# Another order for the steps of an attention stage spread over four slots, in a fused attention and mixture-of-experts kernel

## The chip, the cores and the metric

The kernel runs on one NeuronCore of a Trainium2 chip. The time is the device time of one execution in microseconds (us). The kernel before takes 812.54 us, the median of three runs (812.51 to 813.44).

## What is computed

Eight batches of 576 tokens, eight heads of 64. Attention is causal over a window of 128 with a linear bias by distance; its output, 512 wide per token, goes to a mixture of eight experts, of which each token uses one. A token may keep the expert of the token before it.

```python
scores = scale * q @ k.T + bias                 # where 0 <= i - j < 128, else -1e9
attn = exp(scores - max); attn = attn / (sum(attn) + 1e-9)
x = attn @ v                                     # heads side by side: 512 per token
...
e = argmax(x[s] @ w_gate) if s == 0 or sigmoid(x[s] @ w_local) < 0.5 else e_of_the_token_before
out[s] = softmax(x[s] @ w_gate)[e] * (relu(x[s] @ w1[e]) @ w2[e])
```

## The kernel before, in words

The attention handles one **pair** of heads at a time: 8 batches x 4 pairs = 32 pairs. Each pair is cut into nine score tiles of 128 rows and 128 or 192 columns. The work on a pair is a set of small steps, methods of `Scores` (L475) and `Weigh` (L530), each a letter and a number:

- S0 to S4 (TensorE, PE): the score matmuls, into four PSUM banks; 34 per pair.
- D0 to D8 (VectorE, DVE): one fused instruction per tile adds the bias, writes the tile `scs` and reduces the row minimum to `mn`; a second, short one reads that out.
- E0 to E8 (ScalarE, ACT): the exponential into the pair's probability buffer `pb` (name `cut`, two of them), with the row sums in `sm`.
- N3 and N8 (L523): the normalisation of tiles 0 to 3 and of 4 to 8. GpSimd (POOL) adds 1e-9 to the sums, VectorE takes the reciprocal `r`, GpSimd multiplies each tile by it.
- U0 to U3 (TensorE): transposes of the probabilities into PSUM tiles `pt` (two); C0 to C3 copy them to `pts`, C3 on VectorE, the others on ScalarE.
- M0 to M4 (TensorE): the matmuls with v, into one PSUM bank `xa`, first for columns 0 to 383, then for the rest; X0 and X1 (ScalarE) copy these to `xT`.
- T0 and T1 (VectorE): 32x32 transposes into the one tile `T`. After T1 of a batch's fourth pair the sync engine's queue (SP) stores all of `T` to `xd` in device memory (L600).

Each engine runs its instructions strictly as written: `InOrder` (L156) chains them, and so most of the attention has the one line L162 in the profile. The order is written by hand: `ORDER` (L60) has one string for each of the four pairs of a batch. The loop over **slots** (L834) runs one string per slot; a step with no mark belongs to this slot's pair, each mark `'` moves it to an earlier pair, and for the steps of `Weigh` one pair more. So the work on one pair lies in slots 0 to 3 from its start (`DEPTH`, L66).

The routing of a finished batch goes in between: a `.` in the string lets the generators `tokens` and `route` (L605, L625) take one step: logits by matmul, the largest of them, a scan over the tokens that carries the held expert on (`hr`), ranks, tables (`tbl`). Nine of these steps put matmuls on TensorE into the one PSUM tile `pk`, each between a VectorE or ScalarE step that feeds it and another that reads it. After the last pair the experts' matmuls follow (L1007 to L1009), with fp32 operands split in two parts (L237, L239).

Of the kernel before, what the change touches and what calls it, by code (L numbers as in the profile page):

```python
# [10 lines left out]
F32 = mybir.dt.float32  # L11
# [39 lines left out]
def windows(nb):  # L51
# [13 lines left out]
]  # L65
DEPTH = 3  # L66
# [8 lines left out]
def moe_attention(ctx, tc, qT, kT_d, vv, wg, wl, w1, w2, out):  # L75
# [232 lines left out]
    with ExitStack() as actx:  # L308
        sp = actx.enter_context(tc.tile_pool(name="asmall", bufs=2))
        ap = actx.enter_context(tc.tile_pool(name="aconst", bufs=1))  # L310
        psc = actx.enter_context(tc.tile_pool(name="psc", bufs=4, space=PS))
# [15 lines left out]

        def load(b):
            (q, q7), v = Q[b % 2], V[b % 2]
            k = sh.tile([P, 4, S], F32, name="kr")  # L330
            for p in range(4):
# [7 lines left out]
                if p == (2 if b == 0 else 1):  # L339
                    nc.sync.dma_start(v[0], vv[b, 0:512].rearrange("(j p) c -> p j c", p=P))  # L340
                    nc.sync.dma_start(v[1][0:64], vv[b, 512:S])
# [133 lines left out]
        class Scores:  # L475


            def __init__(self, b, p, q, q7, k):
                self.p, self.q, self.q7, self.k, self.pb = p, q, q7, k, PB[(4 * b + p) % 2]
                self.mn = sp.tile([P, 9], F32, name="mn")  # L480
                self.sm = sp.tile([P, 9], F32, name="sm")
                self.r = sp.tile([P, 9], F32, name="r")
                self.ps, self.sc = {}, {}
# [4 lines left out]
            def scores(self, i):  # L488
                bank, at = BANK[i]
                return self.ps[bank][:, at:at + self.width(i)]  # L490

            def S(self, j):
                for bank in {0: (0, 1), 2: (2, 3)}.get(j, ()):
                    self.ps[bank] = psc.tile([P, 512], F32, name="sc")
# [813 lines left out]
```

## Time and profile before

| | |
|---|---|
| median of three runs | 812.54 us |
| the profiled execution: its own time, its span | 811.47 us, 809.6 us |
| attention, until the last store of `T` is issued | 338.3 us of the span |
| busy share of the span | PE 90%, DVE 62%, ACT 53%, POOL 50% |
| mean granted clock of TensorE | 0.929 |

The busy share of TensorE is the mean of two stages. The attention ends at 338 us; from 388 us on the experts' matmuls fill TensorE. What the change touches is read from the windows before 338 us, batch by batch. A batch here is the time from one store of `T` to the next.

### The profile page before, as it was taken

Reading aid. Unit: us, or ns where it says so; the run is one execution under the profiler, and the core shown is the slowest. Engines: PE = TensorE matmul, PEld = TensorE weight load, DVE = VectorE, ACT = ScalarE, POOL = GpSimd, SP = SyncE. Lnnn points to the kernel's source line nnn. Section 1 sums busy time; section 2 is a strip of 40 time slices with the busy share of each in tenths; the row PEclk is TensorE's granted clock in tenths of the full one; section 3 lists DMA queues with packets and bytes.
Section 4 is the critical chain, followed back from the end, with each engine's and each line's share of the span. In section 5 each row is a group of like instructions: output and inputs, shape, how many; then the busy total and the mean of one; then the engine's idle time right before and its main releaser. Section 6 shows DMA issues by size and latency. Waiting matters only on the chain.

```text
span 809.6 us, 15889 instructions
## 1 busy us (share of the span) xinstructions
PE 725.5 (90%) x5210; PEld 582.9 (72%) x5210; DVE 500.2 (62%) x1731; ACT 428.4 (53%) x1202; POOL 406.7 (50%) x671
## 2 busy tenths in 40 slices
PE   6788888777787878996999999999999999999996
PEld 3555555545565555675898888898999998888995
DVE  4444656565565566899966459756657657456661
ACT  3576666676666665751454334535545546345550
POOL 8663435343434474677355707365647636705410
PEclk7797979999987887997999999999999999999998
DMA  9343434363625321574455536556657657535520
GB/s 298 112 130 112 148 95 144 107 179 92 188 61 158 130 59 29 168 245 145 143 173 168 167 98 201 177 165 196 220 146 222 213 165 222 175 111 174 187 95 18
DMA packets 65815, 122.20 MB, mean 151 GB/s; under 512 B 14050, under 2 KB 33122, under 8 KB 65731
## 3 DMA queue, kind: packets, MB, share of 16 engines
q1 hardware_dynamic: 55906, 101.27, 40.2%
q0 software_dynamic: 9392, 19.31, 8.1%
q8 instruction: 42, 0.69, 0.3%
q10 hardware_dynamic: 432, 0.59, 0.2%
q14 instruction: 43, 0.34, 0.1%
HBM read 102.14 MB, written 20.30 MB: 151 GB/s over the span
## 4 chain that ended last, share of the span: by engine, by line
PE 61%; ACT 15%; DVE 9%; POOL 6%; issue 6%; DMA 2%; POOLq 0%; ACTq 0%; DVEq 0%
ACT cut L162 11%; PE y L1009 9%; PE y L1008 9%; PE y L1007 9%; PE h L1009 8%; PE h L1007 8%; PE h L1008 8%; PE pt L162 3%; ACT pts L162 3%; PE xa L162 3%; PE sc L162 2%; POOL cut L162 2%; PE pk L162 2%; DMA xd<-T 2%; DVE scs L162 1%
## 5 line engine op out<-in xcount | busy, mean ns | idle before, releaser
L177 POOL DMA_INDIRECT kr<-xd,xidx x142 | 155.9, 1098 | 51.8 <-issue 42.1
L239 DVE TENSOR_TENSOR cut<-wraw,cut 128x512 fp32r<-128x512 f32 x231 | 150.1, 689 | 44.5 <-ACT cut L237 43.1
L162 ACT ACTIVATE cut<-scs,mn 128x192 f32<-128x192 f32 (+1 forms) x288 | 125.0, 436 | 58.4 <-DVE mn L162 47.5
L237 ACT CAST cut<-wraw 128x512 fp32r<-128x512 f32 x218 | 124.2, 618 | 50.1 <-PE y L1009 50.0
L1007 PE MATMUL h<-qx,cut 128*128 128x384 f32 (+7 forms) x472 | 149.6, 317 | 0.0
L1009 PE MATMUL h<-qx,cut 128*128 128x384 f32 (+7 forms) x472 | 149.3, 316 | 0.0
L1008 PE MATMUL h<-qx,cut 128*128 128x384 f32 (+7 forms) x472 | 148.9, 315 | 0.0
L1009 PE MATMUL y<-cut,hl 128*128 128x512 f32 x328 | 129.5, 395 | 0.4 <-DVE hl L1056 0.3
L1008 PE MATMUL y<-cut,hh 128*128 128x512 f32 x328 | 129.4, 394 | 0.0
L1007 PE MATMUL y<-cut,hh 128*128 128x512 f32 x328 | 129.2, 394 | 0.0
L162 POOL TENSOR_SCALAR cut<-cut,r 128x192 f32<-128x192 f32 (+1 forms) x288 | 114.7, 416 | 22.2 <-DVE r L162 13.6
L994 POOL DMA_INDIRECT out<-y,sidx x41 | 43.2, 1054 | 161.4 <-ACT y L1016 133.8
L1055 ACT ACTIVATE hh<-h 128x384 fp32r<-128x384 f32 (+7 forms) x114 | 50.2, 440 | 131.7 <-PE h L1009 131.6
L1056 DVE SCALAR_TENSOR_TENSOR hl<-h,hh 128x384 fp32r<-128x384 f32 (+7 forms) x120 | 58.6, 489 | 83.1 <-ACT hh L1055 81.0
L1007 PEld LDWEIGHTS h<-qx,cut 128*128 128x128 f32 x472 | 90.1, 191 | 5.7
L1008 PEld LDWEIGHTS h<-qx,cut 128*128 128x128 f32 x472 | 89.9, 190 | 5.5
L162 PE MATMUL xa<-pts,cut 128*64 128x128 f32 (+2 forms) x640 | 82.8, 387 | 12.0 <-ACT pts L162 11.9
L1009 PEld LDWEIGHTS h<-qx,cut 128*128 128x128 f32 x472 | 89.9, 190 | 1.8
L162 PE MATMUL pt<-ident,cut 128*128 128x128 f32 x512 | 81.6, 308 | 6.9 <-POOL cut L162 5.1
L162 PEld LDWEIGHTS pt<-ident,cut 128*128 128x128 f32 x512 | 66.9, 159 | 25.9 <-POOL cut L162 18.9
L162 POOL TENSOR_SCALAR r<-sm 128x4 f32<-128x4 f32 x64 | 12.4, 194 | 144.2 <-ACT cut L162 140.9
L162 PE MATMUL sc<-kr,qx 64*64 64x192 f32 (+2 forms) x1088 | 81.9, 369 | 1.6 <-DVE mn L162 1.4
(203 smaller groups left out, 1039.4 us busy)
## 6 DMA issues: line engine op xcount, KB each, us to landing
wraw<-w SPq DMA_DIRECT2D x120, 512.0 KB
xd<-T SPq DMA_DIRECT2D x8, 1152.0 KB
kr<-kT SPq DMA_DIRECT2D x31, 288.0 KB
qx<-qT SPq DMA_DIRECT2D x30, 288.0 KB
cut<-v SPq DMA_DIRECT2D x8, 1024.0 KB
kr<-xd,xidx POOLq DMA_INDIRECT x142, 3.8
qx<-qT SPq DMA_DIRECT2D x16, 64.0 KB
v<-v SPq DMA_DIRECT2D x8, 128.0 KB
```

The costliest lines, as they stand in the source:

```text
L162: ins = getattr(self.engine, name)(*args, **kw)
L177: queued(nc.gpsimd.indirect_dma_start(out=r, out_offset=None, in_=src[0:n, :], in_offset=bass.IndirectOffsetOnAxis(ap=col, axis=0), bounds ...
L237: scalar.copy(c[:, 0, f], raw[:, f])
L239: (pool if 2 * n + f == POOL_CUT else vector).tensor_tensor(c[:, 1, f], raw[:, f], c[:, 0, f], ALU.subtract)
L994: ins = nc.gpsimd.indirect_dma_start(out=out[:, :], out_offset=bass.IndirectOffsetOnAxis(ap=col, axis=0), in_=y, in_offset=None, bounds_ch ...
L1007: nc.tensor.matmul(o, ah, bh, start=start, stop=False)
L1008: nc.tensor.matmul(o, ah, bl, start=False, stop=False)
L1009: nc.tensor.matmul(o, al, bh, start=False, stop=stop)
L1055: now.act.activation(hh, hp, AF.Relu)
L1056: nc.vector.scalar_tensor_tensor(hl, hp, 0.0, hh, ALU.max, ALU.subtract)
```

## The change

Four things change at once.

- The four strings of `ORDER` are new, and a pair's work now lies in slots 0 to 4 (`DEPTH` 4). N is three kinds of step: A (the addition on GpSimd), R (the reciprocal), P (one multiplication per tile). S2 to S4 move from the next slot into the pair's own; E0 to E3 move from the own slot into the next; A, R and P come a slot later than N did; U0, U1, C0, C1, C3, M, X and T one slot later each.
- `ON_VECTOR = {"C0", "X1"}` replaces the test `j == 3`: C0 and X1 run on VectorE, and C3 goes from VectorE to ScalarE.
- `T` is stored in two pieces: columns 0 to 383 after T0 of the fourth pair, the rest after its T1, a slot later. The load of v (`load_v`) comes one slot later than that of q and k.
- M's first and last flags go by whichever step comes first, and every PSUM bank of the scores has a name of its own with one buffer.

```diff
 ORDER = [
...
-    "T1'' S2' S3' S4' . D5' D8' E5' D4' U2' E8' C2' U3' D6' E4' D7' E6' M0' E7' C3' M1' N8' M2' S0 S1 X0' U0 U1 T0' D0 D2 C0 E0 D1 E2 C1 M3' D3 E1 M4' E3 N3 X1' .",
...
+    "C3''' M0''' M1''' E2' M2''' U1'' D8' A8'' E3' D5' X0''' R8'' U0'' . T1'''' P5'' E1' D4' P6'' P7'' D6' E0' T0''' E8' P8'' C1'' E5' D7' M4''' P4'' M3''' . A3' S0 S1 S2 C0'' D2 R3' S3 E4' X1''' E6' E7' . D3 P2' D1 U2'' P1' P0' D0 U3'' C2'' S4 P3'",
...
-DEPTH = 3
+ON_VECTOR = {"C0", "X1"}
+DEPTH = 4
...
-            def N(self, i):
-                g = slice(0, 4) if i == 3 else slice(4, 9)
-                pool.tensor_scalar(self.r[:, g], self.sm[:, g], 1e-9, 1.0, ALU.add, ALU.mult)
-                dve.reciprocal(self.r[:, g], self.r[:, g])
-                for j in range(g.start, g.stop):
-                    pool.tensor_scalar(self.part(j), self.part(j), self.r[:, j:j + 1], 1.0, ALU.mult, ALU.mult)
+            def A(self, g):
+                pool.tensor_scalar(self.r[:, self.group(g)], self.sm[:, self.group(g)], 1e-9, 1.0, ALU.add, ALU.mult)
+            def R(self, g):
+                dve.reciprocal(self.r[:, self.group(g)], self.r[:, self.group(g)])
+            def P(self, i):
+                pool.tensor_scalar(self.part(i), self.part(i), self.r[:, i:i + 1], 1.0, ALU.mult, ALU.mult)
...
-                (dve.tensor_copy if j == 3 else act.copy)(o, self.pt.pop(j).rearrange("k h (x c) -> k h x c", c=P))
+                (dve.tensor_copy if f"C{j}" in ON_VECTOR else act.copy)(o, self.pt.pop(j).rearrange("k h (x c) -> k h x c", c=P))
...
             def T(self, j):
...
+                lo, hi = ((0, 12), (12, SB))[j]
+                dve.transpose(T[:, lo:hi, self.p], self.xT[:, self.p, 32 * lo:32 * hi].rearrange("p (b i) -> p b i", i=32))
+                if self.p == 3:
+                    at = self.b * XR
+                    nc.sync.dma_start(xd[at + P * lo:at + P * hi].rearrange("(b q) c -> q b c", q=P),
+                                      T[:, lo:hi].rearrange("p b k j -> p b (k j)"))
```

**VectorE, one slot.** The numbers behind the names tell the pairs apart: a pair has its own `mn` and `r`, numbered together (`mn_578` and `r_580`; `mn_540` and `r_542`). ISA is the D step. The rows that read out `mn` are left out. Before:

```order
L162 RECIPROCAL r_466<-r_466 128x5
L162 STREAM_TRANSPOSE T_160<-xT_215 128x12x32
L162 ISA scs_662,mn_578<-sc_640,slopes_137 128x192
L162 ISA scs_664,mn_578<-sc_640,slopes_137 128x192
L162 ISA scs_669,mn_578<-sc_641,slopes_137 128x192
L162 ISA scs_676,mn_578<-sc_641,slopes_137 128x192
L162 RECIPROCAL r_580<-r_580 128x4
L162 STREAM_TRANSPOSE T_160<-xT_215 128x6x32
L162 ISA scs_706,mn_578<-sc_696,slopes_137 128x128
```

And now:

```order
L163 ISA scs_620,mn_540<-sc0_603,slopes_137 128x192
L163 RECIPROCAL r_429<-r_429 128x4
L163 COPY xT_215<-xa_594 128x192
L163 ISA scs_631,mn_540<-sc1_605,slopes_137 128x192
L163 ISA scs_634,mn_540<-sc1_605,slopes_137 128x192
L163 ISA scs_643,mn_540<-sc0_603,slopes_137 128x192
L163 ISA scs_670,mn_540<-sc3_615,slopes_137 128x192
L163 ISA scs_674,mn_540<-sc3_615,slopes_137 128x128
L163 RECIPROCAL r_429<-r_429 128x5
L163 STREAM_TRANSPOSE T_160<-xT_215 128x6x32
```

Before, the reciprocal of pair 580 stood right behind the last D step of the same four tiles, with the exponentials and the addition on other engines in between. Now the reciprocals between the D steps of pair 540 are those of the pair before it, and the copy X1 stands on VectorE.

**ScalarE, from the end of one slot into the next.** ACTIVATE is the E step; `pts<-pt` is C, `xT<-xa` is X. Before:

```order
L162 COPY pts_666<-pt_713 128x2x2x128
L162 ACTIVATE cut_140,sm_579<-scs_711,mn_578 128x128
L162 ACTIVATE cut_140,sm_579<-scs_725,mn_578 128x192
L162 ACTIVATE cut_140,sm_579<-scs_728,mn_578 128x192
L162 COPY xT_215<-xa_731 128x384
L162 COPY pts_780<-pt_765 128x2x2x128
L162 ACTIVATE cut_143,sm_692<-scs_776,mn_691 128x192
L162 ACTIVATE cut_143,sm_692<-scs_778,mn_691 128x192
L162 COPY pts_780<-pt_770 128x2x2x128
```

And now:

```order
L163 COPY pts_703<-pt_751 128x2x2x128
L163 COPY pts_703<-pt_760 128x2x256
L163 ACTIVATE cut_143,sm_654<-scs_734,mn_653 128x192
L163 ACTIVATE cut_143,sm_654<-scs_746,mn_653 128x192
L163 COPY xT_215<-xa_783 128x384
L163 ACTIVATE cut_143,sm_654<-scs_749,mn_653 128x192
L163 ACTIVATE cut_143,sm_654<-scs_758,mn_653 128x192
L163 ACTIVATE cut_143,sm_654<-scs_796,mn_653 128x192
L163 COPY pts_844<-pt_791 128x2x2x128
L163 ACTIVATE cut_143,sm_654<-scs_800,mn_653 128x128
```

C2 and C3 now stand back to back at the slot's border, all nine E steps of one pair lie between there and the next C2, and X1 is gone from ScalarE.

**SP, around the store of a batch.** Before:

```order
L334 DMA qx_135<-qT 128x576
L340 DMA cut_141<-v 128x4x512
L341 DMA v1_142<-v 64x512
L600 DMA xd_75<-T_160 128x18x128
L334 DMA qx_135<-qT 128x576 x3
```

And now:

```order
L340 DMA qx_135<-qT 128x576
L611 DMA xd_75<-T_160 128x12x128
L331 DMA cut_141<-v 128x4x512
L332 DMA v1_142<-v 64x512
L611 DMA xd_75<-T_160 128x6x128
L340 DMA qx_135<-qT 128x576 x2
```

The first two thirds of `T` go out ahead of the load of v, the last third behind it.

## Rows read from the trace of the kernel before

**Rows 1.** Busy time by window (the queries for stretches of the span). The first line is a slot without routing, the next five each run from one store of `T` to the next, the last three are the way over to the experts' stage. Columns: the stretch and its length, busy us of each engine (x instructions), granted clock of TensorE, DMA share, GB/s.

```profile
41.93:49.97 8.04, 6.77 (x83) 4.81 (x82) 4.03 (x24) 6.06 (x23) 5.74 (x17) 1.00 0.68 227
...
58.66:99.78 41.12, 33.51 (x339) 22.46 (x338) 24.04 (x129) 26.11 (x97) 18.14 (x70) 0.83 0.43 130
99.78:140.53 40.75, 33.58 (x342) 22.62 (x338) 23.62 (x128) 26.11 (x97) 16.35 (x46) 0.83 0.40 122
140.53:178.32 37.79, 28.67 (x342) 19.56 (x338) 23.42 (x128) 25.99 (x97) 16.33 (x46) 1.00 0.44 130
178.32:216.57 38.25, 29.80 (x342) 20.30 (x338) 23.21 (x128) 26.00 (x97) 16.14 (x46) 0.96 0.42 131
216.57:257.48 40.91, 34.27 (x346) 23.52 (x338) 23.82 (x128) 26.24 (x97) 16.60 (x46) 0.83 0.36 111
...
338.30:360.00 21.70, 20.56 (x142) 16.09 (x138) 19.92 (x57) 12.77 (x30) 16.64 (x13) 1.00 0.88 286
360.00:388.00 28.00, 20.63 (x117) 16.80 (x115) 26.26 (x111) 8.39 (x17) 19.66 (x19) 0.82 0.45 138
388.00:809.60 421.60, 414.05 (x2266) 367.80 (x2263) 257.34 (x514) 193.80 (x376) 204.03 (x190) 0.99 0.53 164
```

**Rows 2.** The transposes into `T` and their stores over the whole span: durations in ns (least, median, most), start of the first and of the last.

```profile
L162 DVE STREAM_TRANSPOSE T<-xT x64: 345/459/578, 29.2 to 337.9; 128x384 f32<-128x384 f32 x32, 128x192 f32<-128x192 f32 x32
L600 SPq DMA_DIRECT2D xd<-T x8: 377/378/387, 58.7 to 338.3; - x8
```

**Rows 3.** The chain of work that ended last, inside the slot without routing from 41.93 to 49.97 us: start, us, what.

```profile
42.20 0.25 DVE scs L162
...
42.87 0.62 ACT cut L162 x3
43.50 0.47 ACT pts L162
43.97 1.28 ACT cut L162 x6
45.24 0.08 issue
45.32 0.21 POOL r L162
45.53 0.02 issue
45.55 0.20 DVE r L162
45.75 0.08 issue
45.84 1.92 POOL cut L162 x5
```

**Rows 4.** Who waited for whom in the batch from 140.53 to 178.32 us: engine and tile, what it waited for: us in total, times, longest us.

```profile
DVE r L162 <- POOL r L162: 11.5, 8, 2.1
ACT pts L162 <- PE pt L162: 4.6, 4, 2.2
...
PE pk L162 <- DVE tbl L162: 2.5, 1, 2.5
PE pk L162 <- DVE hr L162: 2.3, 2, 1.9
...
PE pk L162 <- DVE rcb L162: 1.6, 1, 1.6
...
PE pk L162 <- DVE ro_all L162: 1.4, 2, 0.9
...
PE xa L162 <- ACT pts L162: 1.1, 2, 0.6
DVE T L162 <- DMA xd<-T: 1.0, 1, 1.0
```

**Rows 5.** Groups of instructions by shape in the same batch: count, busy us, mean ns of one, idle time before them.

```profile
L162 ACT COPY pts<-pt 128x512 f32<-128x512 f32 x12 | 6.8, 570 | 4.6 <-PE pt L162 4.6
...
L162 DVE CUSTOM_DVE_ANT_0 scs<-sc,slopes 128x192 f32<-128x192 f32 x24 | 7.5, 344 | 0.0
...
L162 DVE COPY pts<-pt 128x512 f32<-128x512 f32 x4 | 2.7, 686 | 0.0
...
L162 ACT COPY xT<-xa 128x192 f32<-128x192 f32 x4 | 1.2, 297 | 0.0
```

**Rows 6.** The chain of work that ended last, around the second store of `T`: start, us, what.

```profile
99.78 7.08 DMA xd<-T
...
106.96 0.58 DVE T L162
```

**Rows 7.** Busy time by window, columns as in Rows 1: two stretches right before the granted clock fell, and the two that followed them at the lower clock.

```profile
66.80:70.20 3.40, 1.51 (x10) 1.01 (x10) 1.59 (x13) 2.54 (x10) 0.19 (x1) 1.00 0.36 94
70.20:80.40 10.20, 8.47 (x66) 5.62 (x70) 5.99 (x30) 6.22 (x23) 4.07 (x12) 0.50 0.00 1
...
107.80:111.20 3.40, 1.63 (x12) 1.13 (x10) 1.51 (x12) 2.55 (x10) 0.42 (x2) 0.99 0.35 89
111.20:121.40 10.20, 8.80 (x70) 5.96 (x74) 5.68 (x27) 6.54 (x25) 3.54 (x10) 0.50 0.01 2
```

More of the change, by code (lines that the diff above doesn't have):

```diff
@@ L338, in load @@
                         nc.sync.dma_start(q7[hs, :, hs], qT[b, :, hs, 448:512].rearrange("p d q -> d p q"))
-                if p == (2 if b == 0 else 1):
-                    nc.sync.dma_start(v[0], vv[b, 0:512].rearrange("(j p) c -> p j c", p=P))
-                    nc.sync.dma_start(v[1][0:64], vv[b, 512:S])
+                if p == 2 and b == 0:
+                    load_v(b)
             return q, q7, k, v
@@ L479, in __init__ @@
                 self.p, self.q, self.q7, self.k, self.pb = p, q, q7, k, PB[(4 * b + p) % 2]
-                self.mn = sp.tile([P, 9], F32, name="mn")
-                self.sm = sp.tile([P, 9], F32, name="sm")
-                self.r = sp.tile([P, 9], F32, name="r")
+                self.mn, self.sm, self.r = (sp.tile([P, 9], F32, name=n, bufs=4) for n in ("mn", "sm", "r"))
                 self.ps, self.sc = {}, {}
@@ L489, in scores @@
                 bank, at = BANK[i]
+                if bank not in self.ps:
+                    self.ps[bank] = psc.tile([P, 512], F32, name=f"sc{bank}")
                 return self.ps[bank][:, at:at + self.width(i)]
             def S(self, j):
-                for bank in {0: (0, 1), 2: (2, 3)}.get(j, ()):
-                    self.ps[bank] = psc.tile([P, 512], F32, name="sc")
                 if j == 4:
@@ L572, in M @@
             def M(self, j):
+                half = j // 3
+                first = half not in self.o
+                if first:
+                    self.o[half] = pxa.tile([P, 512], F32, name="xa")
+                o = self.o[half]
                 if j == 0:
-                    self.xa = pxa.tile([P, 512], F32, name="xa")
-                    self.mult(self.xa[:, 128:384], 4, 4, 1, True, False)
+                    self.mult(o[:, 128:384], 4, 4, 1, first, False)
                 elif j == 1:
-                    self.mult(self.xa[:, 256:384], 8, 2, 2, False, False)
+                    self.mult(o[:, 256:384], 8, 2, 2, first, False)
@@ L587, in X @@
             def X(self, j):
+                copy = dve.tensor_copy if f"X{j}" in ON_VECTOR else act.copy
                 if j == 0:
-                    act.copy(self.xT[:, self.p, 0:384], self.xa[:, 0:384])
+                    copy(self.xT[:, self.p, 0:384], self.o[0][:, 0:384])
                 else:
-                    act.copy(self.xT[:, self.p, 384:S].rearrange("p (s q) -> p s q", q=64),
-                             self.xb[:, 0:192].rearrange("p (s q) -> p s q", q=64)[:, ::-1])
+                    copy(self.xT[:, self.p, 384:S].rearrange("p (s q) -> p s q", q=64),
+                             self.o[1][:, 0:192].rearrange("p (s q) -> p s q", q=64)[:, ::-1])
@@ L613, in tokens @@
                 yield
-                act.copy(part[:, lo:lo + n], pk[:, :n])
+                (dve.tensor_copy if "part" in ON_VECTOR else act.copy)(part[:, lo:lo + n], pk[:, :n])
                 yield
@@ L787, in early, with over @@
             known.append(e)
+        def over(kind, n):
+            return all((a, n) in emitted for a in atoms if a[0] == kind)
         def gathers():
@@ L803, in turns @@
             for t in range(r.n):
-                while taken.count(t) < 4 or ("S4", 4 * NB - 5) not in emitted:
+                while taken.count(t) < 4 or not over("S", 4 * NB - 5):
                     yield
@@ L812, in turns @@
             yield from W.split(tp.tile([P, 2, 2, DM], F32R, name="xT"), act, dve)
-            for what in (("M4", 4 * NB - 5), ("U3", 4 * NB - 2), ("M4", 4 * NB - 1)):
-                while what not in emitted:
+            for what in (("M", 4 * NB - 5), ("U", 4 * NB - 2), ("M", 4 * NB - 1)):
+                while not over(*what):
                     yield
                 yield from W.split(W.room(), act, dve)
-        known, taken, routed, read, emitted = [], [], [], [], []
+        known, taken, routed, read, emitted = [], [], [], [], set()
         rows0 = [Rows(4 * KS * e, KS * e, 4 * k, idx0, n) for e, (k, n) in enumerate(EARLY)]
@@ L821, in moe_attention @@
         pairs = {}
+        atoms = {a.strip("'") for a in ORDER[0].split()}
         LATE = 4 * EARLY[0][1] + 4
@@ L864, in moe_attention @@
                 loaded = load(b + 1)
+            if p == 2 and b + 1 < NB:
+                load_v(b + 1)
         run(chain(prep[";"], prep[":"], prep[","], side))
```

37 lines of the change are left out of this document (17 added, 20 removed), and 6 rows, old and new, of the table ORDER.

## The prediction

> **What bounds the kernel now.** I read the busy time by window first, since the change touches the attention alone. The experts' stage has TensorE busy for 414.05 of its 421.60 us [rows 1]: nothing there can be gained by another order ahead of it, but an attention that ends sooner lets it begin sooner. The attention is the part before the last store at 338.3 us; the eight stores lie between 58.7 and 338.3 [rows 2], so a batch takes (338.3 - 58.7) / 7 = 39.95 us. In no window of a batch is an engine full: in the one with the granted clock at 1.00 throughout, TensorE is busy for 28.67 of 37.79 us, ScalarE 25.99, VectorE 23.42, GpSimd 16.33 [rows 1]. So the batch is bound by waits between engines, not by an engine.
>
> Which waits, the chain of one slot without routing tells [rows 3]: D on VectorE, the exponentials on ScalarE, then the addition on GpSimd (0.21), the reciprocal on VectorE (0.20), the five multiplications on GpSimd (1.92). The table of waits shows the price in a batch: VectorE stands for 11.5 us in front of its eight reciprocals [rows 4], which is most of its idle 37.79 - 23.42 = 14.4 us. VectorE works strictly in its order, so the next D steps, and with them the next exponentials, stand behind each reciprocal. That is a ring: E, A, R, D, E. The routing's VectorE steps stand behind it too, and TensorE then waits for them: 2.5 + 2.3 + 1.6 + 1.4 = 7.8 us, and 1.1 for C [rows 4], together 8.9 of its 9.1 idle us.
>
> **The change, part by part.**
>
> *A, R and P apart, a slot later.* The instructions and their number stay the same. Between the last E of a group and its A, and between A and R, there are now steps of other pairs on each of the three engines, so R should find its sums ready: I take the 11.5 us as gone from VectorE's path. Bounds: nothing of it goes if A is late on GpSimd (it stands behind the four P of the group before), all of it goes if A is on time. GpSimd is busy for 16.33 of 37.79 us [rows 1], so I take the second. P is then followed by U half a slot later or more; GpSimd's 1.92 us for five tiles [rows 3] fits there.
>
> *Copies.* X1 leaves ScalarE: -4 x 0.297 = -1.2 us a batch [rows 5]. On VectorE it costs between 0.344 (an instruction of the same 128x192 from PSUM) and 0.686 us (a copy of 128x512) [rows 5]; I take 0.37, near the one of the same width: +1.5 us a batch, at most +2.7. C0 comes to VectorE and C3 goes to ScalarE: both are 128x512, 0.686 and 0.570 us each [rows 5], so the swap costs neither engine anything. The sums per batch become ScalarE 25.99 - 1.2 = 24.8, VectorE 23.42 + 1.5 = 24.9. Both stay below TensorE's 28.67, and that covers the copies; if TensorE's floor were lower, they would be the next bound.
>
> *The store in two pieces.* The second store took 7.08 us and T0 of the next pair began right after it [rows 6]; VectorE's wait for it in the full-clock batch is 1.0 us [rows 4]. Now each piece has until the same T step of the next pair, a slot later. A slot without routing is 8.04 us now [rows 1] and I expect some 7 after; two thirds of the store need about 4.7 (estimate, in proportion to 7.08). So the wait goes; it is inside VectorE's idle time, and I count nothing for it by itself. Eight more DMAs on SP cost it 8 x 0.38 = 3 us in all [rows 2], on a queue that waits for others most of the time. What stands behind the second piece are loads of q for a batch that is four slots away.
>
> *One slot more.* A fifth slot for each pair adds a drain slot at the end. Its last steps are M, X and T alone, and the experts' first matmuls may run beside them; at the start, S and D of more pairs run ahead while GpSimd still builds the bias tables. I count 0, bounds -2 and +4 us (half a slot of 8.04).
>
> *The sum.* TensorE becomes the fullest engine: 28.67 us per batch at the full clock. Of its waits I keep the two that are round trips through the one tile `pk` and that no order shortens, the table (2.5) and the scan (2.3): 28.67 + 4.8 = 33.5 us. The others (1.6 + 1.4 + 1.1) were VectorE and ScalarE running late, and go. Over the seven batches between the stores: 7 x (39.95 - 33.5) = 45.2 us. The slots before the first store have no routing: from the first T at 29.2 to 58.7 [rows 2] there are three and a half, of 8.04 us, with TensorE busy for 6.77 [rows 1]; at 7.2 they give 3.5 x 0.84 = 2.9. Together 48.1 us. The hand-over to the experts, 338 to 388 us, is led by VectorE (26.26 of 28.00 busy in its second part [rows 1]) with work that the change leaves alone, so it moves forward as a whole. Against the profiled execution: 811.47 - 48.1 = 763.4; it stands 1.07 below the median of the runs, so 764.5 against that. I say **764**.
>
> *A rule weighed.* That sum takes TensorE's matmul time as a floor. The same rows show its weight loads busy for only 19.56 of the 37.79 us [rows 1]. The Trainium skill (Perfetto Trace Analysis, Identifying the Most-Contended Engine) says that matmul busy time is a poor measure of how near TensorE is to its limit, and that the busy share of the weight loads should be used instead. By that rule TensorE has more room than I gave it, and the sum would go by VectorE's 24.9; that is the first rival.
>
> **The rivals.**
>
> 1. *TensorE's floor is lower than its busy time.* Then the batch is VectorE's 24.9 us plus the same 4.8 of round trips: 29.7 us, a gain of 7 x 10.25 + 3 = 75, time **738**. For it: the busy time overlaps and may hold waits. Against it: in the experts' stage the matmuls are 98% busy and nothing else bounds there, and three engines with 24.8 to 28.7 us of work each would have to interlock with 5 us of slack.
>
> 2. *The clock still falls.* In three of the five batches the granted clock is 0.83 on average, which is one third of the time at 1.2 GHz instead of 2.4, and they take 40.75 to 41.12 instead of 37.79 us [rows 1]. Before each fall TensorE was busy for only 1.51 and 1.63 of 3.40 us [rows 7]; it was waiting for the routing's `rcb`, and then ran at the lower level for 10 us. If such gaps remain, a batch costs 40.75 - 37.79 = 3.0 us more: 36.5, a gain of 7 x 3.45 + 3 = 27, time **785**. At worst TensorE's full extra busy time counts, 33.58 - 28.67 = 4.9 [rows 1]: 38.4, time 799. For it: the routing keeps its gaps of some 2 us in one place. Against it: TensorE has less idle time around them. The Trainium skill (TensorE: Matmul & The Clock Gate, A second HAM failure mode: psum-queue depth-cycling) describes a kernel whose short idle spells between groups of matmuls keep sending the clock back and forth; by that rule this rival is what happens, and the rows of the batches at 0.83 agree with it, the one at 1.00 does not.
>
> 3. *Slower: the routing waits grow.* The new order fills ScalarE and VectorE (24.8 and 24.9 us) and the routing's steps are still thrown in by the same dots, in the same strict queues. Nine of them put matmuls on TensorE. Now six of the waits show up, 7.8 us, 1.3 each [rows 4]. If all nine wait as long, and C's waits grow by as much as they are, the waits are 9 x 1.3 + 2 x 1.1 = 13.9: a batch of 42.6, 7 x 2.65 - 3 = 16 us slower, time **828**. It decides from 39.95 - 28.67 = 11.3 us of TensorE waits a batch on; they are 9.1 now. For it: each of the steps has a reader on a queue that is now fuller. Against it: what made them late, 11.5 us of reciprocals, is what the change takes out.
>
> 4. *The change does not do what it says.* A is behind the P steps on GpSimd, R still waits for it, and a ring of the same length stays with one slot more: **812** to 816.
>
> **How the numbers follow.** My forecast, a batch of 32 to 35.5 us (750 to 778), has a chance of 0.62; rival 1 0.12, rival 2 0.18, rival 3 0.05, rival 4 0.03. The first three are faster, which makes 0.92. What a measurement can tell from no change is about 0.2%, 1.6 us; rival 4 holds most of what lies within it. The range takes in rival 1 and rival 2 at its first price, with the bounds of the extra slot: 734 to 792. Outside are the worst of rival 2 and rivals 3 and 4, under 2 in 10.
>
> **What would show it.** In the profile after: the distance of the stores of `T` about 33 us; VectorE's wait for `r` of GpSimd near 0 in a batch; TensorE's idle time in a batch about 5 us, with the table and the scan as its leading waits; VectorE busy for about 25 us, ScalarE for a little less; no wait of T for its store; the way from the last store to the full experts' stage about 50 us as now. The prediction is wrong if the reciprocals still wait for some us, if the granted clock in the batches stays near 0.83, or if the distance from the last store to the end grows by what the attention has won.

## The result, and the profile of the changed kernel

The changed kernel takes **722.88 us** (median of four runs, 721.73 to 723.69) against 812.52: a ratio of 0.8907, 95% interval 0.8868 to 0.8946. Here and below a median counts every run, while a ratio leaves out runs over 1.5% above the fastest of their kernel, so that the two need not agree to the last tenth of a per cent. The forecast was 764 with a range of 734 to 792: the sign and the way were right, the gain was nearly twice as large, and the time lies below the range. The profiled execution has a span of 721.1 us against 809.6, 88.5 less, of which the forecast had 48.1.

The transposes into `T` and their stores over the whole span (columns as in [rows 2]); the stores are now two per batch:

```profile
L163 DVE STREAM_TRANSPOSE T<-xT x64: 326/466/579, 30.2 to 250.6; 128x384 f32<-128x384 f32 x32, 128x192 f32<-128x192 f32 x32
L611 SPq DMA_DIRECT2D xd<-T x16: 359/380/388, 48.7 to 251.0; - x16
```

The last store goes out at 251.0 us instead of 338.3. From there to the end of the span it is 721.1 - 251.0 = 470.1 us, and was 809.6 - 338.3 = 471.3 [rows 2]. So 87.3 of the 88.5 us lie in the attention, and the way over to the experts moved forward as a whole.

Busy time by window (columns as in [rows 1]); the first three run from the second store of one batch to that of the next, the last three are the way over and the experts' stage:

```profile
53.17:79.89 26.72, 26.23 (x335) 18.52 (x335) 23.92 (x132) 24.22 (x92) 16.46 (x46) 1.00 0.59 180
...
107.26:134.41 27.15, 26.66 (x340) 18.98 (x339) 23.81 (x132) 24.83 (x94) 16.43 (x46) 1.00 0.59 181
...
161.53:192.09 30.56, 29.20 (x365) 20.35 (x363) 24.94 (x139) 26.50 (x100) 16.36 (x46) 1.00 0.57 176
251.30:272.00 20.70, 19.32 (x132) 15.38 (x132) 18.28 (x53) 12.12 (x27) 14.33 (x13) 1.00 0.80 257
272.00:300.00 28.00, 20.62 (x122) 16.87 (x121) 27.05 (x114) 9.08 (x18) 19.88 (x19) 0.88 0.46 140
300.00:721.10 421.10, 413.25 (x2260) 366.92 (x2258) 256.43 (x513) 193.28 (x375) 204.95 (x190) 1.00 0.53 164
```

A batch takes 27.15 us where the one at the full clock took 37.79 [rows 1]. TensorE is busy for 26.66 of them, 98%. The other engines' busy times are close to what they were (VectorE 23.42 to 23.81, ScalarE 25.99 to 24.83, GpSimd 16.33 to 16.43): the same work, without the holes. Note TensorE's own: about the same number of matmuls at the same granted clock, yet 28.67 us before and 26.66 now. Its busy time before was not all work. The batch at 161 us has 365 matmuls instead of 340, as preparation for the experts comes in; the two behind it take some 31 and 28 us.

The chain of work that ended last, in the batch from 107.26 us (shares by line, then the first pieces: start, us, what), is now for the most part TensorE's own queue:

```profile
by line: PE pt L163 26.5%; PE xa L163 22.6%; PE sc L163 19.4%; PE pk L163 12.1%; DVE scs L163 8.7%; DVE ro_all L163 3.7%; DVE T L163 2.7%; issue 1.4%; DVE pts L163 1.2%; DVE r L163 1.0%; DVE tbl L163 0.5%; DVE tz L163 0.3%; DVE mn L163 0.3%
...
107.78 0.25 PE pk L163 x8
108.03 1.23 PE xa L163 x12
109.27 0.59 PE pk L163 x4
109.85 0.87 PE pt L163 x8
110.72 0.11 PE pk L163
110.83 0.81 PE xa L163 x12
111.64 1.35 PE sc L163 x32
113.00 0.31 PE pk L163 x4
113.31 1.02 PE pt L163 x8
```

Up to 126.67 us group follows group with no other engine between; in the chain of before [rows 3] ScalarE, GpSimd and VectorE took turns. The routing's matmuls (`pk`) stand among the attention's. It is not TensorE alone: VectorE has the 5.3 us from 126.68 to 131.98, and in the batch ahead of this one, of nearly the same length, VectorE's D steps (22.4%) and ScalarE's exponentials (13.1%) lead the chain. In the four batches from 53.17 us TensorE's four groups (`pt` 20.2, `xa` 18.1, `sc` 14.8, `pk` 11.7%) make 65% of it; in the four of before from 58.66 us the same four make 18%, and ScalarE's exponentials alone 32.5%.

Who waited for whom, from 50 to 250 us, about seven batches (columns as in [rows 4]); VectorE, then TensorE, then ScalarE:

```profile
DVE L L163 <- PE pk L163: 14.9, 7, 2.9
...
DVE r L163 <- POOL r L163: 1.2, 2, 0.7
...
PE pk L163 <- DVE hr L163: 3.4, 3, 2.4
PE pk L163 <- DVE tbl L163: 2.9, 6, 0.6
...
ACT cut L163 <- DVE mn L163: 0.2, 1, 0.2
```

The reciprocals' wait, 11.5 us in one batch before [rows 4], is 1.2 in seven. The table's, 2.5 in one batch, is 0.4; the scan's (`hr`) is under 0.5. No T waits for its store.

Groups by shape in the batch from 107.26 us (columns as in [rows 5]):

```profile
L163 ACT COPY pts<-pt 128x512 f32<-128x512 f32 x13 | 7.3, 579 | 0.1
L163 DVE COPY pts<-pt 128x512 f32<-128x512 f32 x4 | 2.7, 679 | 0.0
...
L163 DVE COPY xT<-xa 128x192 f32<-128x192 f32 x4 | 1.4, 338 | 0.0
```

X1 on VectorE takes 338 ns (0.37 us was taken), and the copies of 128x512 cost what [rows 5] had for them.

### The profile page after: what moved, and what is told of

Same layout as the page of the kernel before. It is cut to its first block, busy times and chain, and to the rows that moved or that the text cites. A ratio compares the mean times of both kernels' runs of the same rounds, so it can differ in the third digit from the quotient of the medians.

```text
span 721.1 us, 15988 instructions
## 1 busy us (share of the span) xinstructions
PE 678.9 (94%) x5210; PEld 558.0 (77%) x5210; DVE 504.4 (70%) x1763; ACT 419.5 (58%) x1170; POOL 409.3 (57%) x671
## 4 chain that ended last, share of the span: by engine, by line
PE 75%; DVE 10%; POOL 6%; issue 5%; ACT 3%; DMA 1%; POOLq 0%; DVEq 0%
PE y L1025 10%; PE y L1024 10%; PE y L1023 10%; PE h L1023 10%; PE h L1025 9%; PE h L1024 9%; PE pt L163 5%; PE xa L163 5%; PE sc L163 4%; DVE scs L163 3%; PE pk L163 3%; POOL cut L163 2%; ACT cut L163 2%; POOL qx L163 1%; DVE cut L240 1%
## 5 line engine op out<-in xcount | busy, mean ns | idle before, releaser
L163 POOL TENSOR_SCALAR cut<-cut,r 128x192 f32<-128x192 f32 (+1 forms) x288 | 116.4, 422 | 55.9 <-DVE r L163 32.7
L1024 PEld LDWEIGHTS h<-qx,cut 128*128 128x128 f32 x472 | 89.6, 190 | 5.6
L163 PE MATMUL pt<-ident,cut 128*128 128x128 f32 x512 | 73.3, 285 | 10.7 <-POOL cut L163 10.6
L163 PEld LDWEIGHTS pt<-ident,cut 128*128 128x128 f32 x512 | 56.8, 144 | 31.3 <-POOL cut L163 20.3
L1025 PEld LDWEIGHTS y<-cut,hl 128*128 128x128 f32 x328 | 61.5, 188 | 15.3 <-DVE hl L1072 2.0
L163 DVE CUSTOM_DVE_ANT_0 scs<-sc,slopes 128x192 f32<-128x192 f32 x224 | 68.9, 334 | 5.3 <-ACT cut L163 3.4
L163 PE MATMUL xa<-pts,cut 128*64 128x128 f32 (+2 forms) x640 | 70.2, 337 | 0.6 <-ACT xT L163 0.6
```

The lines of the kernel that those rows point to most:

```text
L163: ins = getattr(self.engine, name)(*args, **kw)
L1024: nc.tensor.matmul(o, ah, bl, start=False, stop=False)
L1025: nc.tensor.matmul(o, al, bh, start=False, stop=stop)
```

## The experiments

Every kernel's median is in us, its ratio is to the kernel before, timed with it. In the last three groups of runs the experts' stage took some 60 to 95 us longer in every kernel, in the kernel before too (872.92 to 906.22), while the attention seems not to have: a kernel run in two of these groups, with 561.2 and 536.8 us from its last store to the end, issued its last store at 282.7 and 282.8 us. No kernel was profiled both in one of these groups and outside them. So all kernels are set side by side by the start of the last store of `T` in their profiles. For the store in two pieces alone that does not do: its profile is of a run of 817.36 us at a granted clock of 0.919, far from its median.

| kernel | last store, us | median (of before) | ratio, interval |
|---|---|---|---|
| before | 338.3 | 812.52 | 1 |
| before + store in two pieces | 344.2 | 809.31 (813.34) | 0.9935 [0.9892, 0.9978] |
| before + ring out | 307.5 | 780.44 (813.34) | 0.9608 [0.9572, 0.9645] |
| ... and store in two pieces | 297.5 | 770.59 (811.72) | 0.949 [0.9433, 0.9546] |
| ... and T later | 282.8 | 816.45 (872.92) | 0.933 [0.9255, 0.9405] |
| ... and S2 to S4 ahead | 280.5 | 815.30 (872.92) | 0.9349 [0.9307, 0.9391] |
| changed | 251.0 | 722.88 (812.52) | 0.8907 [0.8868, 0.8946] |
| changed, old copies | 249.3 | 721.19 (813.21) | 0.8877 [0.8823, 0.8931] |
| changed, old copies, T behind X | 266.4 | 803.75 (872.92) | 0.9222 [0.9176, 0.9269] |
| changed, ring back | 262.7 | 734.61 (813.34) | 0.9039 [0.9006, 0.9073] |
| changed, one store | 283.7 | 752.50 (813.21) | 0.9257 [0.9199, 0.9314] |
| changed, ring back, one store | 292.8 | 762.09 (811.72) | 0.937 [0.9313, 0.9428] |
| changed, dots four steps later | 259.0 | 813.02 (906.22) | 0.8994 [0.8902, 0.9086] |
| changed, dots four steps earlier | 256.3 | 811.59 (906.22) | 0.8983 [0.8877, 0.909] |

### The ring of the reciprocals, out and back

Out, in the old order (`mn`, `sm` and `r` have four buffers each there, as in the changed kernel):

```diff
-    ... D5' D8' E5' D4' ... M1' N8' M2' ... C0 E0 D1 E2 ... E3 N3 X1' .
+    ... D5' D8' E5' R3' P0' P1' P2' P3' D4' ... M1' A8' M2' ... C0 E0 R8' P4' P5' P6' P7' P8' D1 E2 ... E3 A3 X1' .
```

> The kernel before, three slots deep as it was, same copies and store; only N is split into A, R and P, and R with its P steps stands later: R3 in the next slot behind two D steps, R8 behind D0, D2 of the next pair. Ring theory: VectorE's 11.5 us a batch in front of the reciprocals go to under 3, and the batch falls from 40 to 33 to 36 us: 770 to 785. Rival (the deeper pipeline is what counts): the waits move to TensorE's U behind P and the time falls by under 10 us (803 to 812).

Back, in the new one:

```diff
-    ... D8' A8'' E3' D5' X0''' R8'' ... E0' ... A3' S0 ... D2 R3' ... E6' E7' D3 ...
+    ... D8' E3' D5' X0''' ... E0' A3' R3' ... S0 ... D2 ... E6' E7' A8' R8' D3 ...
```

> The changed kernel, with A and R put right behind the last exponential of their group again (A3, R3 behind E0; A8, R8 behind E7), all else in its place. Ring theory: VectorE waits again in front of the reciprocals, 6 to 11 us a batch, D and E behind it are late, and the batch goes from 27.2 to 32 to 36 us: 757 to 785. Rival (depth of five slots covers it): under 5 us slower (723 to 728).

Out alone, it gave 32.9 us. Back alone, it cost 11.7. Both theories of the second run missed: the ring costs there, but a third of what it costs in the old order. Waits of VectorE with the ring back, from 60 to 250 us:

```profile
DVE r L163 <- POOL r L163: 10.2, 19, 1.1
```

The reciprocals wait again, yet 10.2 us in 6.6 batches, where the old order had 11.5 in one [rows 4]. My reading is that a reciprocal that waits closes a ring only if ScalarE then waits for the next D. In the new order E0 to E3 come a slot after their D steps, and ScalarE has their results lying ready (its wait for `mn` is 0.2 us above, and with the ring back none is listed), so it goes on and the sums come soon after.

### The store of T

The piece alone in the old order:

```diff
-                    if self.p == 3:
-                        nc.sync.dma_start(xd[self.b * XR:self.b * XR + XR]..., T...)
+                if self.p == 3:
+                    lo, hi, at = ((0, 12), (12, SB))[j] + (self.b * XR,)
+                    nc.sync.dma_start(xd[at + P * lo:at + P * hi]..., T[:, lo:hi]...)
```

> The kernel before, with the store of T in two pieces (columns 0 to 383 after T0 of the fourth pair, the rest after its T1) and nothing else. If the store is a part of the gain by itself, VectorE's wait of T for its store goes, 1.0 us a batch at the full clock and 2.2 us in the batch of the second store: 7 to 15 us faster (798 to 806), the more so since the wait is followed by D and E. If it is hidden in the ring E, A, R, D anyway, 0 to 3 us.

It gave 0.65%, 5.3 us, with an interval of 1.8 to 8.8: between the two cases, and the interval reaches into both. The times of single runs of this kernel spread from 801.15 us at a granted clock of 0.964 to 817.36 at 0.919, so that nothing finer can be read from it. With the ring out it is clearer:

> The kernel before with the reciprocals a slot later (780.4 us) and the store in two pieces. With the ring out alone, VectorE's T waited 2.7 us for its store in a batch. Theory, the wait for the store was covered by the ring and counts as soon as the ring is gone: 7 x 2 to 2.7 us less, 761 to 767. Rival, other waits of the old order take its place: 776 to 781. Far below 761 would say that nothing else of the new order matters.

780.44 fell to 770.59: 9.9 us, where the theory had 14 to 19. What stands in its place is shown below. And taken back from the new order:

```diff
-                if self.p == 3:
+                if self.p == 3 and j == 1:
...
-                                      T[:, lo:hi]...)
+                                      T...)
```

> The changed kernel with one store of T after T1, instead of two pieces. T0 of the next pair then waits for a store that was issued a few us before: the store took 7.08 us before, a slot takes 6.8 us now, and T1 stands about a third of a slot into it. If VectorE's wait is on the path: 3 to 5 us in each of seven batches, 15 to 35 us longer (738 to 758). If the slack of VectorE (3.3 us a batch) takes most of it: 0 to 5 us longer. The prediction counted 0 for this part.

29.6 us longer. VectorE's longest wait in that kernel from 50 to 275 us, and two places of its chain of work:

```profile
DVE T L163 <- DMA xd<-T: 26.6, 7, 5.1
```

```profile
85.35 0.26 DVE T L163
85.63 6.78 DMA xd<-T
92.51 0.58 DVE T L163
...
116.97 0.26 DVE T L163
117.25 7.12 DMA xd<-T
124.47 0.58 DVE T L163
```

T1, the store, T0 of the next pair: the store stands on the path in full, in each of the seven batches (5.51 to 8.04 us); before, it stood there twice, with 7.08 [rows 6] and 6.00. It takes about as long as it did, but T0 now comes sooner after T1: T waits for it seven times, 26.6 us, and before four times, 4.5. The granted clock in these batches is 0.89 to 0.95, where the changed kernel has 1.00 in six of seven, so that a part of the 29.6 us may be the clock; the two were not told apart. The same part that was worth some 5 us in the old order is worth 30 in the new one.

### Ring and store both back

> The changed kernel with both taken back: A and R right behind the exponentials of their group, and one store of T. What is left of the change is the order over five slots and the copies. Theory, the parts add: 734.6 + 29.6 = 764, 758 to 770. Rival 1, they stand in each other's time, since both keep VectorE waiting: 750 to 757. Rival 2, each protected the other and without both the batch falls back to the kernel before: over 780.

762.09: the parts add in the new order (734.61 + 29.6 = 764). So with the ring back the store still costs 27.5 us (762.09 - 734.61). Left over are the order over five slots and the copies, and they alone make 50 of the 89.6 us. What goes with that order, a name of its own for each PSUM bank of the scores and the later load of v, was not tried apart from it.

### The copies, and which engine is full

```diff
-ON_VECTOR = {"C0", "X1"}
+ON_VECTOR = {"C3"}
```

> The changed kernel with the copies on their old engines: X1 and C0 on ScalarE, C3 on VectorE. ScalarE gets 1.2 us a batch more (24.8 to 26.0 of 27.15), VectorE 1.4 less. The prediction's view (the copies are covered by TensorE): 0 to 3 us longer. Rival, ScalarE at 26 of 27.15 us has no slack for its place in the order, so that the copies were a needed part of the gain: 5 to 12 us longer, 728 to 735.

721.19: the copies are no part of the gain; ScalarE's 1.2 us more a batch was hidden, and VectorE's 1.4 less gave nothing that can be told. This version and the changed one can't be told apart (their intervals overlap); no better version came out of the experiments.

More work for one engine at a time in the changed kernel: S4's matmul issued twice, T1's transpose made twice, a further copy of 192 columns on ScalarE.

```diff
-                    pe.matmul(self.scores(6), ...)
+                    for _ in range(2):
+                        pe.matmul(self.scores(6), ...)
```

> The changed kernel with the score matmul of step S4 issued twice per pair, into the same place: TensorE gets two more matmuls of 192 columns per pair (one step S4 holds one call; some 0.33 us a pair at the rate of its neighbours, 32 pairs: 10.6 us in all), the other engines nothing. Theory, TensorE is now what bounds the attention: 8 to 12 us longer, 731 to 735 against 722.9. Rival, a ring of waits or VectorE or ScalarE bounds it and TensorE has room: 0 to 3 us longer.

```diff
-                dve.transpose(T[:, lo:hi, self.p], ...)
+                for _ in range(1 + j):
+                    dve.transpose(T[:, lo:hi, self.p], ...)
```

> The changed kernel with the 32x32 transpose of step T1 made twice: VectorE gets one more instruction of 0.34 us per pair, 10.9 us over 32 pairs. Theory, TensorE bounds: VectorE goes from 23.8 to 25.2 us of work in a batch of 27.15 us, so it is hidden: 0 to 3 us longer, at most 726. Rival, VectorE bounds or lies on a ring: 8 to 11 us longer, 731 to 734.

```diff
                     copy(self.xT[:, self.p, 0:384], self.o[0][:, 0:384])
+                    copy(self.xT[:, self.p, 0:192], self.o[0][:, 0:192])
```

> The changed kernel with one more copy of 192 columns on ScalarE per pair, right behind X0: 0.30 us a pair, 9.5 us over 32 pairs. VectorE and TensorE, given about as much, each became 5.3 us longer, half of it. Theory, the three engines are so full that each one's work counts: 4 to 6 us longer, 727 to 729. Rival, ScalarE has room (it took 1.2 us a batch more with the old copies at no cost): 0 to 2 us, 721 to 725.

Measured 728.14, 728.31 and 723.51. Four batches of each, store to store, first the changed kernel, then with more for TensorE, for VectorE and for ScalarE (columns as in [rows 1]):

```profile
53.17:161.53 108.36, 106.42 (x1349) 75.46 (x1349) 95.45 (x528) 98.72 (x371) 65.67 (x181) 1.00 0.59 180
```

```profile
52.75:164.85 112.10, 110.77 (x1383) 81.37 (x1382) 95.26 (x528) 98.52 (x372) 65.69 (x181) 1.00 0.58 175
```

```profile
52.84:165.08 112.24, 107.23 (x1344) 75.91 (x1344) 100.85 (x544) 99.89 (x372) 65.82 (x181) 1.00 0.57 175
```

```profile
51.96:160.15 108.19, 106.33 (x1351) 75.67 (x1351) 95.43 (x528) 101.61 (x388) 65.98 (x181) 1.00 0.60 181
```

TensorE's added work was less than I had put down: 4.35 us of busy time in four batches, where 16 pairs at 0.33 are 5.3. Of it 3.74 us appear in the time, 86%. So TensorE has next to no room in these batches. But of VectorE's 5.40 us 3.88 appear too, 72%, although VectorE is idle for 12% of the time: it has slack in sum and little at the places where TensorE needs its result (TensorE's weight loads for `sc` waited 5.6 us for `mn` there). The two set the pace together, as in the chain above. ScalarE's extra copies are 16 of 319 ns in four batches, 5.1 us, and those batches take 108.19 us against 108.36: nothing of it appears. The expectation that VectorE's would be hidden was wrong.

This holds for these four batches. From the fifth on, up to the last store, the changed kernel, then with more for TensorE and for VectorE:

```profile
161.53:251.00 89.47, 79.65 (x924) 56.38 (x922) 76.28 (x388) 71.84 (x253) 59.69 (x130) 0.98 0.46 143
```

```profile
164.85:254.90 90.05, 81.88 (x942) 59.53 (x940) 75.44 (x388) 71.63 (x252) 59.56 (x130) 0.98 0.45 142
```

```profile
165.08:256.30 91.22, 80.17 (x920) 56.85 (x919) 80.42 (x400) 71.66 (x252) 58.94 (x130) 0.96 0.45 140
```

TensorE is busy for 89% there, and of its 2.23 us more 0.58 appear, of VectorE's 4.14 us 1.75 (and of ScalarE's 2.72 us 1.08): these three batches still wait for other things. Over the whole kernel the two additions cost 5.3 and 5.4 us, not the 8 to 12 that a full TensorE would have made of its own.

### What of the order over five slots does it

With ring and store settled, the old order has a batch of 34.34 us (columns as in [rows 1]):

```profile
157.84:192.19 34.35, 29.36 (x339) 19.72 (x338) 23.60 (x128) 25.76 (x97) 16.36 (x45) 1.00 0.47 143
```

VectorE's waits in it from 60 to 250 us:

```profile
DVE T L162 <- ACT xT L162: 31.8, 27, 1.7
DVE hr L162 <- ACT hold L162: 9.5, 12, 1.1
```

T stands right behind X, and VectorE's queue behind T. Moved apart in the old order, and together in the new one (with old copies):

```diff
-    T1'' S2' ... D6' E4' ... T0' D0 D2 ... D3 E1
+    S2' ... D6' T1'' E4' ... D0 D2 ... D3 T0' E1
```

> The kernel before with the reciprocals a slot later and the store in two pieces (770.6 us), and now T0 and T1 put some steps further behind X0 and X1: T0 behind D3 instead of ahead of D0, T1 behind D6 of the next slot instead of at its head. VectorE waited for xT for 31.8 us in the 190 us from 60 to 250, 5.7 in a batch of 34.3. Theory, these waits are on the path and are what the longer distances of the new order remove: 2 to 5 us less in each of seven batches, 735 to 757. Rival, the waits move on to the next steps, since in the old order every engine waits for every other: 764 to 772.

> The same kernel as with T moved alone. Its first run was on another chip, on which the experts' stage took 90 us longer in every kernel; its last store of T was issued at 283 us of the span. If the attention is the same on both chips: last store at 281 to 285 us, time 750 to 757.

```diff
-    ... X0''' R8'' U0'' . T1'''' ... E0' T0''' ... X1''' E6' ...
+    ... X0''' T0''' R8'' U0'' . ... E0' ... X1''' T1''' E6' ...
```

> The changed kernel with the copies on their old engines (721.2 us), and T0 and T1 put right behind X0 and X1, as near as in the old order. VectorE then waits in front of T for ScalarE. Theory, the distance of T from X is a main part of what the order over five slots gives: 2 to 6 us more in each of seven batches, 735 to 763. Rival, the slack of VectorE (some 4 us a batch here) takes it: 721 to 727.

> The same kernel as the changed one with old copies and T right behind X. Its last store of T was at 267.5 us on the other chip, against 249.3 in the kernel without this edit. If the attention is the same on both chips: time 736 to 742, 15 to 20 us over 721.2.

The times expected of the two second runs were missed by some 60 us, since the experts' stage was long again. The last store came 15 us earlier in the first (297.5 to 282.8; 844.23 and 816.45 us, 0.9354 and 0.933 of the kernel before), 17 to 18 us later in the second (249.3 to 266.4 and 267.1; 833.42 and 803.75). So this one distance is worth 15 to 18 us in either order. In its place, in the old order, came VectorE's wait for TensorE:

```profile
DVE scs L162 <- PE sc L162: 25.1, 23, 3.1
DVE hr L162 <- ACT hold L162: 7.3, 12, 0.9
```

which the next edit took aim at:

```diff
-    S2' S3' S4' . D5' ... U0 U1 D0 ...
+    . D5' ... U0 U1 S2 S3 S4 D0 ...
```

> The old order with the reciprocals a slot later, the store in two pieces, T0 and T1 further behind X0 and X1, and now S2, S3 and S4 ahead of M3 and M4 in TensorE's queue, behind U1 of their own slot, as the new order has them in the own slot. With T moved alone a batch took 31.7 us and VectorE's longest wait was scs for sc, 25.1 us in 190, 4.2 in a batch. Theory, the gain of the new order is a sum of such lengthened distances: this takes 1.5 to 4 us more off a batch, 10 to 28 us off the time with T moved alone (that was 0.935 of the kernel before, about 753 to 760 here), so 728 to 748. Rival, the wait moves on: within 5 us of the kernel with T moved alone.

The wait fell, the time hardly (last store 282.8 to 280.5): the rival was right. In the same 190 us it is now

```profile
DVE L L162 <- PE pk L162: 11.1, 11, 1.8
DVE scs L162 <- PE sc L162: 9.3, 12, 1.1
DVE hr L162 <- ACT hold L162: 7.7, 12, 0.9
DVE oh_all L162 <- PE pk L162: 4.9, 6, 0.9
```

many small waits on several engines, and the batch looks like this:

```profile
147.41:178.82 31.41, 29.40 (x339) 19.44 (x340) 23.24 (x129) 25.55 (x98) 16.41 (x46) 1.00 0.51 156
```

TensorE is "busy" for 29.40 of 31.41 us with as many matmuls as take 26.66 in the changed kernel. (The profiles of T moved alone and of this kernel are of runs of 821.35 and 824.72 us, above their medians.) The other 30 us, from 280.5 to 251.0, I have not split further: what is left in the new order is E0 to E3, the whole of U, C and M at longer distances from what feeds them, and the dots. That E0 to E3 are the part which keeps ScalarE from waiting fits its wait for `mn` (8.1 us in 190 in this kernel, 0.2 in 200 in the changed one), but it was not tried alone.

### The places of the routing's steps

Each dot four places later, or earlier, for example in the second string:

```diff
-    ... R8'' U0'' . T1'''' P5'' E1' D4' P6'' ...
+    ... R8'' U0'' T1'''' P5'' E1' D4' . P6'' ...
```

> The changed kernel with every dot (a step of the routing) four steps later in its string, all else the same. The new strings also set the dots anew, which the prediction overlooked: it kept 4.8 us a batch for the round trips of the table and the scan, and 0.5 was left. Theory, these places are fitted to the order: the round trips come back with 2 to 5 us a batch, the last store of T goes from 251 to 265 to 286 us, ratio to the kernel before 0.907 to 0.93. Rival, with a full TensorE queue any place will do: last store 250 to 256, ratio 0.888 to 0.897.

> The same with every dot four steps earlier. The same two cases: 265 to 286 us for the last store if the places are fitted, 250 to 256 if any place will do. Both could be wrong in one direction only: a dot that is later gives the step before it more time and the next one less, so that only one of the two moves may cost.

Last stores at 259.0 and 256.3: 8.0 and 5.3 us later, some 1 us a batch, much less than the 2 to 5 that the theory had, a little more than the rival's bound. A batch of the first, and what it shows TensorE waiting for from 50 to 250 us, where the changed kernel has 0.2:

```profile
83.01:111.64 28.63, 27.16 (x342) 18.93 (x338) 23.85 (x133) 25.11 (x93) 16.36 (x46) 1.00 0.58 173
```

```profile
PE pk L163 <- DVE rcb L163: 5.9, 6, 1.4
```

So the places are fitted, but most of the round trips' time is gone at any place. The medians do not show this cost: against the kernel before, timed with them, the two gain 93.2 and 94.6 us, and the changed kernel gained 89.6, each on its own occasion, with intervals of 8 us and more for the first two.

### The clock

```diff
+                if lo == 0:
+                    for _ in range(12):
+                        pe.matmul(busy[:, :P], ident, ident, start=True, stop=True)
                 pr = ptk.tile([1, 512], F32, name="pk")
```

> The kernel before, with twelve matmuls of 128x128 on TensorE ahead of the one that waits for rcb, once a batch; their result is not used. If the lower clock that follows this wait costs what the batches show (40.75 against 37.79 us), the falls behind it go, the mean granted clock rises from 0.93 to 0.96 or more and the kernel is 8 to 15 us faster (798 to 805). If the clock is only a follower of the waits, or the falls come from other gaps, the time stays within 3 us or rises by up to 7 x 1.6 = 11 us.

812.69 us (810.26 to 815.81), ratio 0.9994, interval 0.9971 to 1.0018; the granted clock rose from 0.929 to 0.962 in the two profiles, and the last store moved from 338.3 to 336.4. So the time did not follow the clock here. In the runs of the kernel with two stores it did, by 11.7 us over 0.029 (812.86 us at 0.935, 801.15 at 0.964), and in those of the kernel before timed with this one by 9.5 us over 0.022 (816.37 at 0.925, 806.87 at 0.947). In the trace the added matmuls are busy for 20.0 us in seven batches, where the kernel before waited 12.0 us for `rcb`:

```profile
L162 PE MATMUL pk<-ident 128*128 128x128 f32 x168 | 20.0, 276 | 0.0
```

The 8.0 us between may have eaten what the clock gave back. Yet at a granted clock of 1.00 a batch takes 37.93 us with them and 37.79 without, and batches at 0.92 take 40.24 and 40.92, nearly as long as those at 0.83 before, 40.75 to 41.12. Whether the clock made these batches long or followed their waits, and so what it was worth in the kernel before, stays open.

## Why the prediction was wrong in size

**What bounds.** Right: waits between engines, with the ring as the longest. **A, R, P apart.** Right that the wait goes. That it is 11.5 us a batch said little of its worth: 7 x 11.5 = 80 us, but 32.9 when taken out alone and 11.7 when put back.

**The sum** failed, in its floor: TensorE's 28.67 us a batch and the 4.8 of round trips on top. Measured are 26.66 us busy in 27.15, with 0.5 of idle time. Of the 40.4 us between forecast (48.1) and result (88.5), this term is 7 x (33.5 - 28.3) = 36.4, where 28.3 is the mean of the seven batches, (251.3 - 53.17) / 7; the slots before the first store gave 5.5 us instead of 2.9, and the way over 1.2.

- The 28.67 was taken from the busy time of a kernel whose TensorE kept waiting. The same work shows 29.36 to 29.40 us in the old order with ring out, and 26.66 in the new, all at a granted clock of 1.00. My reading is that short waits count as busy there: the ends of matmuls in the records are modelled, and the records overlap (in the batch of [rows 5] 64 `pt` matmuls of 277 ns each make 8.6 us of busy time), so that a gap shorter than a record can vanish in it. That was not shown by itself. I had put this down as the first rival (738) and gave it 0.12, arguing from the experts' stage, where matmuls follow each other without waits. There busy time is work; in the attention not all of it was.
- The 4.8 were kept as round trips that "no order shortens". A round trip costs TensorE nothing as long as its queue holds other work in between: 0.5 us of idle time a batch was left of 4.8, and moving the dots either way brought back about 1 us.

The Trainium skill (Perfetto Trace Analysis, Identifying the Most-Contended Engine) had warned that matmul busy time is a poor measure of how near TensorE is to its limit; the trace agrees, with the numbers just given, though the Trainium skill's reason there, that pipelined instructions look smaller in a trace, would make the busy time too small, and here it was too large. The measure that was weighed in its place, the busy share of the weight loads, would not have given the limit either: it is 18.98 of 27.15 us, 70%, in batches in which 86% of TensorE's added work appeared in the time.

**One slot more**, counted 0 within -2 and +4, was the second failure, and the larger one in kind. Ring and store together give 770.59 in the old order, with a batch of 34.34 us: close to the forecast's 33.5 and 764. So what I had priced is about what these two give (by luck in part, since the store was counted at nothing), and I took the new order for a mere drain slot. But it is what removes the waits that come after them, and 47.7 us lie there: 15 to 18 of them go with the distance of T from X, and some 30 were not split, so that their cause stays open.

**The store** was rightly seen to go, wrongly counted at nothing: the idle time that covered it went too. It was the ring's in the smaller part (5.3 us with the ring, 9.9 with the ring out, both in the old order) and the old order's other waits in the larger: in the new order the store costs 27.5 us even with the ring back. I had named that cover and not asked what the store costs without it: 29.6 us.

**The copies**: right, hidden (721.19 with the old ones); VectorE's total came out at 23.81 us a batch, not 24.9, since the rest of its work took 1.0 us less, for a reason that was not looked for. **The way over** moves as a whole: right, 471.3 and 470.1 us. **The clock**: it is 1.00 in six of the seven batches and 0.94 in the last, so the second rival (785) did not come about. The Trainium skill's rule that was weighed there, short idle spells that send the clock back and forth (TensorE: Matmul & The Clock Gate, A second HAM failure mode: psum-queue depth-cycling), speaks of a kernel with such spells, and the changed one has 0.5 us of idle time a batch. **Slower** (828) presumed that the routing's waits grow with fuller queues; they fell, and stayed at about 1 us a batch more with the steps moved four places either way.

**The range** did not reach far enough down because even its fastest case kept the 4.8 us of round trips. Its ends are not worked out to the last: the first two rivals with the extra slot's bounds of -2 and +4 give 736 and 789, not 734 and 792. Nor is 1.6 us what a measurement can tell: nineteen runs of the kernel before lie between 806.87 and 816.37.

## What to carry to other kernels

A floor for an engine must not be read from its busy time in a kernel where it waits: look for a stretch where its work follows without a gap, or give it a little more work and see how much of it appears, stretch by stretch. When a change takes out the longest wait, price the waits that it covered as if they stood alone (here a store: 5 us before, 30 after), since a change that removes several at once gains more than each does by itself. A step's distance from the one that feeds it, across queues that run strictly in order, can be worth more than work that is moved from engine to engine: T behind X cost 15 to 18 us without one instruction more, and the moved copies gave nothing that can be told.

## What the runs showed of the hardware that was not expected

The records' busy time of TensorE for the same matmuls of a batch, at a granted clock of 1.00, was 26.66, 27.14, 28.67 or 29.40 us, by the order alone. And in the four batches from the second store on, an engine idle for 12% of the time (VectorE) passed 72% of added work on, while one idle for 9% (ScalarE) passed on nothing: idle share did not tell which engine has room. Why the experts' stage took some 60 to 95 us longer on some occasions, in every kernel run then, was not found. It does not go with the chip: one chip gave the kernel before 813.34 us in one group of runs and 872.92 in a later one.
